# A new hand-written order for a recurrence and a token-mixing MLP on one core: pair 0's v and k are loaded ahead of q, and the cast of wk reads at a stride

## The chip, the core and the metric

The kernel runs on one core of a Trainium2 chip. The core has a matmul engine (PE, with its weight loads shown apart as PEld), a vector engine (DVE), a scalar engine (ACT), a general engine (POOL), and SP, which here only issues DMAs. Each engine takes its instructions strictly in the order of its own queue. The metric is the device time of one execution in microseconds (us); the time before is the median of three runs.

## What is computed

Per head, a linear attention with a decaying state; its output, heads side by side, is the input of a mixing layer over tokens. Batch 4, 8 heads, 768 tokens, head size 64, so the model width is 512; `d_hyper` is 64.

```python
gamma = 1.0 - 2.0 ** (-5.0 - np.arange(H))
for t in range(S):
    state = gamma * state + einsum('bhd,bhe->bhde', k[:, :, t], v[:, :, t])
    y[:, :, t] = scale * einsum('bhd,bhde->bhe', q[:, :, t], state)
x = y.transpose(0, 2, 1, 3).reshape(B, S, H * D)
wq, wk = x @ w_q, x @ w_k
W_tok = 1 / sqrt(d_hyper) * einsum('bsd,btd->bst', wq, wk)
mixed = einsum('bst,btd->bsd', W_tok, x)
return np.maximum(mixed, 0.0) @ w_out
```

## The kernel before

The recurrence is done in chunks of 128 tokens. Two chunks make a pair, three pairs a batch, twelve pairs (0 to 11) the whole. Inside a chunk the scores of q and k are masked and multiplied with v; what came before the chunk enters through the state. The mixing layer needs no 768 x 768 matrix: per batch it forms z, which is wk's transpose times x, and then multiplies it with wq.

All sums of PE go to eight banks. Bank 7 holds the running state; banks 0 to 6 are given to the steps by hand. Inputs land in 27 slots of a buffer called `stage` (one 512 KB load each), and outputs leave from slots too.

The order of everything is one string, `ORDER`. A word in it is a step, with its pair, its part, the engine behind a colon (A for ACT, V for DVE, P for POOL) or the banks behind an @ (a letter a or b after them takes half of two banks), and a slot behind =. So `cv.0.1:P` scales chunk part 1 of v of pair 0 on POOL, and `trk.2@12a` transposes k of pair 2 into halves of banks 1 and 2. A loop at the end of the kernel runs through the words and issues each step's instructions, so every engine's queue has them in the order of the words. Waits are set where data or a bank needs them. The steps, in the order in which one pair meets them, with the lines of the kernel before:

- `Lk Lq Lv` load k, q, v of a pair (L193, L172; v of kind M in four DMAs at L185; kind N at L178), `LW` the two small weights (L200), `LO` a half of w_out (L207).
- `ck cq` cast k and q to bf16, `cv` scales v by decay factors and casts (L419; L400 for kind 2; L410 for kinds M and N). Casts and copies are at L147 on ACT and at L148 on DVE and POOL.
- `trk trq` transpose k and q on PE, wide (8 matmuls, one bank) or split (16 small ones, halves of two banks); `ek eq` copy the result out.
- `sc` scores (L597, L583 for kind 2), half the heads each; `eat` masks them (L615, DVE).
- `st` adds a chunk to the state (L631); `es` copies the state out.
- `in` the state's share of the output (L670), `ia` the masked scores times v (L724, L710 for kind 2), `ex` scales both to x (L745, DVE).
- `xt` and `exT` transpose x; `W` casts w_q and w_k (in `W`, the second at L344), `WO` a half of w_out.
- `wqk` gives wq and wk of a pair (L787, L798), `ew` copies them out as m; `zm` and `ez` z of a batch (L824); `mx` the mixing (L843), `r` the relu (L861 on ACT, L863 on DVE), `pj` the output projection (L868), `eo` copies it to a slot, `S` stores it (L218).
- `fill` issues matmuls on a tile of zeros that nothing reads (L355).

`KINDS` has a letter for each pair: how its k and v lie on the partitions. R reads two tokens of 64 floats as one row, 2 keeps these pairs of tokens side by side through the whole step, M lays v out so that one instruction scales a part, N takes tokens in plain order. The load named by `FIRST` is issued ahead of the string, in two halves, one from ACT's queue and one from SP's.

Of the kernel before, what the change touches and what calls it, by code (L numbers as in the profile page):

```python
# [17 lines left out]
Lq.2=6 ck.0.1:A trq.0@0 eq.0:A trk.0@1 Lk.2=7 cq.1.0:A ek.0:A ck.1.1:A fill.11@2 sc.0.1@01 st.0.0
ck.1.0:P es.0.0:A Lv.2=8 cv.1.1:P cq.2.1:P Lk.3=9 Lq.3=10 cv.1.0:P eat.0.1:V LW=11 Lv.3=12 cq.2.0:P
trq.1@2 trk.1@34a st.0.1 sc.0.0@56 cv.2.0:P ek.1:V eat.0.0:V cv.2.1:P fill.4@0 in.0.1@01 cq.3.0:P  # L20
Lk.4=13 ck.3.0:P eq.1:A sc.1.0@23 sc.1.1@45 ck.2.1:A ck.2.0:A Lq.4=14 es.0.1:V eat.1.0:V ia.0.1@01
fill.1@6 st.1.0 ia.0.0@01 fill.3@6 trq.2@6 es.1.0:V eat.1.1:V fill.2@2 trk.2@5 eq.2:A ek.2:A
in.1.1@34 st.1.1 LO.0=15 fill.2@2 sc.2.1@56 cv.3.0:P ck.4.0:P cv.3.1:P Lv.4=16 es.1.1:A ex.0:V
LO.1=17 eat.2.1:V sc.2.0@01 st.2.0 in.1.0@34 eat.2.0:V xt.0@2 cq.3.1:A es.2.0:A ck.3.1:A exT.0:A
Lk.5=18 W:A cv.4.1:P fill.1@5 ia.1.1@34 cv.4.0:P ia.1.0@34 in.2.1@56 ia.2.0@56 ex.1:V ia.2.1@56
trq.3@0 in.2.0@56 fill.1@1 xt.1@4 wqk.0@3 eq.3:A trk.3@2 Lq.5=19 ex.2:V exT.1:V ck.4.1:A ek.3:V
xt.2@01a exT.2:V wqk.1@4 fill.1@5 sc.3.1@56 sc.3.0@01 ew.1:A cq.4:A wqk.2@2 ew.0:V Lv.5=20 Lq.6=21
Lk.6=22 Lv.6=23 ew.2:A cq.5:P eat.3.0:V eat.3.1:V st.3.0 zm.0.0@3 zm.0.1@3 trk.4@01a Lq.7=24 trq.4@2
cv.5.0:P ek.4:V WO.0:A ez.0:A es.3.0:A mx.1@34 r.1.0:A cv.5.1:P WO.1:A ia.3.1@56 Lk.7=25 in.3.1@56
ia.3.0@56 st.3.1 ck.6.0:P mx.0@01 eq.4:V r.1.1:V r.0:A Lq.8=26 sc.4.0@23 pj.1.0@4 Lv.7=0 es.3.1:V  # L30
ex.3:V ck.5.0:A ck.5.1:A pj.0.1@0 eo.0.1:A=1 Lk.8=3 eo.1.0:V=2 xt.3@1 eat.4.0:V pj.1.1@4 exT.3:V
sc.4.1@23 mx.2@56 st.4.0 trq.5@0 es.4.0:A trk.5@1 cv.6.0:P st.4.1 ck.7.0:P eat.4.1:V r.2.1:V
eo.1.1:A=2 ek.5:A r.2.0:A cv.6.1:P ia.4.0@34 ia.4.1@34 in.4.1@34 in.4.0@34 Lv.8=4 Lk.10=5 eq.5:V
es.4.1:V pj.0.0@2 cq.8.1:P sc.5.1@56 sc.5.0@01 cq.6:A eo.0.0:A=1 st.5.0 ex.4:V eat.5.1:V eat.5.0:V
ck.6.1:A es.5.0:A Lq.10=6 trq.6@3 pj.2.1@2 xt.4@6 cv.7.0:P cv.7.1:P ck.8.1:P exT.4:V in.5.0@45
in.5.1@45 ia.5.1@45 ia.5.0@45 Lq.9=7 eo.2.1:A=8 eq.6:V wqk.3@2 trk.6@01a wqk.4@3 ex.5:V xt.5@45a
cq.7:A ew.3:A ew.4:A Lk.9=10 st.6.0 ek.6:V exT.5:V sc.6.0@01 eat.6.0:V pj.2.0@6 eo.2.0:V=8 ck.7.1:A
es.6.0:A wqk.5@5 trq.7@01a trk.7@34a ew.5:A sc.6.1@56 zm.1.0@2 cv.8.0:P zm.1.1@2 Lv.9=9 ek.7:V
eq.7:A cq.8.0:A ez.1:A eat.6.1:V sc.7.0@01 st.6.1 mx.3@23 in.6.1@45 r.3.0:A es.6.1:A r.3.1:A
eat.7.0:V ck.10.0:P ia.6.0@45 ia.6.1@45 trq.8@6 ex.6:V cq.10.1:P cv.8.1:P st.7.0 mx.4@01 sc.7.1@23  # L40
ck.8.0:A eat.7.1:V xt.6@4 pj.3.1@5 eq.8:V eo.3.1:V=11 es.7.0:A r.4:A Lq.11=13 ia.7.0@23 ia.7.1@23
in.7.0@23 in.7.1@23 trk.8@01a ex.7:V exT.6:A Lv.10=14 pj.3.0@6 cq.9:P st.7.1 ek.8:A sc.8.0@01
sc.8.1@23 es.7.1:V eo.3.0:A=11 eat.8.0:V mx.5@45 st.8.0 r.5.1:A es.8.0:V r.5.0:V pj.4.1@6 ck.10.1:A
eo.4.1:A=15 wqk.6@0 cq.10.0:A pj.4.0@1 eat.8.1:V ew.6:V ck.9.1:P cv.9.0:P trk.10@6 cv.9.1:P
trq.10@45a xt.7@23a cv.10.0:P Lk.11=12 eo.4.0:A=15 eq.10:V exT.7:V in.8.0@01 in.8.1@01 ia.8.0@01
ia.8.1@01 cv.10.1:P pj.5.0@4 trq.9@5 ek.10:A ex.8:V eq.9:V ck.9.0:A ck.11.0:P Lv.11=17 sc.10.1@23
trk.9@01a pj.5.1@6 eo.5.0:A=16 cv.11.0:P ek.9:A xt.8@45a eat.10.1:V eo.5.1:V=16 sc.9.1@01 eat.9.1:V
sc.9.0@23 cq.11.0:A eat.9.0:V exT.8:A st.9.0 wqk.7@6 wqk.8@4 cq.11.1:A cv.11.1:P ew.7:A es.9.0:A
sc.10.0@01 zm.2.0@6 ew.8:A st.9.1 zm.2.1@6 es.9.1:A ez.2:A trq.11@23a st.10.0 eat.10.0:V in.9.1@45
es.10.0:A ck.11.1:A mx.8@01 eq.11:V r.8.1:V ia.9.0@45 ia.9.1@45 ia.10.1@23 r.8.0:A st.10.1  # L50
in.10.1@23 trk.11@01a in.10.0@23 ia.10.0@23 pj.8.1@6 ex.9:V ek.11:A sc.11.0@01 es.10.1:A ex.10:V
eo.8.1:A=18 sc.11.1@45 xt.9@23a eat.11.0:V st.11.0 pj.8.0@6 exT.9:A es.11.0:A S.3 eat.11.1:V mx.6@01
in.11.0@23 in.11.1@23 r.6.1:A eo.8.0:A=18 ia.11.0@23 r.6.0:V ia.11.1@23 mx.7@45 xt.10@01a ex.11:V
pj.6.1@6 exT.10:A xt.11@2 exT.11:A wqk.9@3 wqk.10@0 ew.10:A eo.6.1:A=19 r.7.1:A r.7.0:V wqk.11@2
ew.9:V pj.6.0@3 ew.11:A zm.3.0@6 zm.3.1@6 eo.6.0:A=19 ez.3:V pj.7.1@2 mx.10@01 r.10.0:V mx.11@56
mx.9@34 eo.7.1:A=21 pj.7.0@2 r.10.1:A pj.10.1@0 S.0 S.4 eo.7.0:A=21 r.11.0:A pj.10.0@1 eo.10.1:A=20
eo.10.0:A=20 S.5 S.8 S.2 r.11.1:V S.6 pj.11.1@2 S.1 r.9:V S.7 eo.11.1:V=22 pj.11.0@0 pj.9.0@1 S.10.1
# [19 lines left out]
def kernel(  # L77
# [255 lines left out]
    wqk_sb = const_pool.tile([128, NDM, 3 * DH], BF16, name="wqk_w")  # L333
    wout_sb = const_pool.tile([128, NDM, DM], BF16, name="wout_sb")

    def W(e):
# [6 lines left out]

        nc.scalar.mul(  # L344
            out=wqk_sb[:, :, 2 * DH :].rearrange("p a (u t) -> p a t u", u=U),
            in_=st[:, 1].rearrange("p a (t u) -> p a t u", u=U),
            mul=float(wk_scale),
        )

# [593 lines left out]
```

## Time and profile before

| | |
|---|---|
| median of 3 runs | 96.33 us (95.49 to 97.65) |
| the profiled execution | 96.55 us, of which the profile's span is 94.8 |
| granted TensorE clock | 0.994 |
| HBM read, written | 20.19 MB, 6.29 MB |

The profile shows one execution. A span's start is 0 us, and "busy" leaves out waiting, branches and DMA issues. A matmul's shown time holds its passage through the array, so several that follow each other overlap; the chain that ended last gives them at the pace at which they follow. In the timeline a row merges neighbours of one kind (x is their count), and the bracket tells how long the engine had been idle and what ended that. POOL's busy time lies between 6 and 71 us, PE's last matmul ends at 91.15.

### The profile page before, as it was taken

How to read it: one execution, taken by the hardware profiler on the slowest of the kernel's cores; microseconds unless marked ns; L12 is line 12 of the kernel's file. 1: busy time of each engine (PE TensorE's matmuls, PEld its weight loads, DVE VectorE, ACT ScalarE, POOL GpSimd, SP SyncE). 2: the span in 40 equal slices, each digit the busy share in tenths (PEclk: the TensorE clock that was granted, in tenths of full speed). 3: DMA queues.
4: the chain of work that ended last, by engine and by line, in shares of the span. 5: the costliest groups of instructions: out<-in, count | busy, mean ns of one | idle time of the engine just before them, and what ended most of it. 6: DMA issues, size and time to landing. Idle time of an engine off the chain costs nothing.

```text
span 94.8 us, 3658 instructions
## 1 busy us (share of the span) xinstructions
PE 84.8 (89%) x1537; PEld 56.7 (60%) x1553; DVE 74.3 (78%) x132; ACT 72.2 (76%) x119; POOL 54.7 (58%) x70
## 2 busy tenths in 40 slices
PE   4989399989989999999999999999999799999940
PEld 1335076657777745868877765676876577644410
DVE  6941999939879999999989998989999976142700
ACT  4444682989999998999687997998977578856450
POOL 6030069599996996999999989999880000000000
PEclk9999999999999999999999999999999999999997
DMA  0999999999999999999679999979599307447983
GB/s 23 321 306 352 318 338 335 325 332 275 335 345 337 359 356 355 293 365 331 129 216 340 392 351 289 323 160 229 126 390 399 142 7 296 154 185 290 406 335 116
DMA packets 38960, 26.71 MB, mean 282 GB/s; under 512 B 10272, under 2 KB 32800, under 8 KB 38944
## 3 DMA queue, kind: packets, MB, share of 16 engines
q1 hardware_dynamic: 38416, 26.22, 87.8%
q10 hardware_dynamic: 528, 0.26, 0.9%
q8 instruction: 12, 0.20, 0.9%
q14 instruction: 4, 0.03, 0.1%
HBM read 20.19 MB, written 6.29 MB: 279 GB/s over the span
## 4 chain that ended last, share of the span: by engine, by line
PE 62%; SPq 14%; DMA 7%; ACT 5%; issue 5%; DVE 4%; DVEq 0%
PE banks L868 22%; SPq L193 10%; DMA stage<-in_q_dram 7%; PE banks L787 6%; PE banks L724 5%; SPq L172 5%; PE banks L597 5%; PE banks L631 3%; PE banks L798 3%; PE banks L843 3%; PE banks L824 3%; PE banks L670 2%; PE banks L546 2%; DVE at L615 2%; PE banks L760 2%
## 5 line engine op out<-in xcount | busy, mean ns | idle before, releaser
L419 POOL TENSOR_TENSOR vs<-stage,fv 64x512 bf16<-64x512 f32 x28 | 29.2, 1043 | 4.2 <-DMA stage<-in_v_dram 1.9
L615 DVE TENSOR_TENSOR at<-banks,maskR 128x1024 bf16<-128x1024 f32 x20 | 23.9, 1218 | 2.3 <-PE banks L597 1.8
L868 PE MATMUL banks<-wout_sb,relu 128*128 128x512 bf16 x85 | 22.1, 381 | 0.7 <-issue 0.3
L147 ACT CAST ks<-stage 64x512 bf16<-64x512 f32 (+1 forms) x26 | 16.0, 616 | 3.4 <-DMA stage<-in_k_dram 3.1
L745 DVE TENSOR_TENSOR x<-banks,fy 128x1024 bf16<-128x1024 f32 x12 | 14.6, 1220 | 0.6 <-PE banks L670 0.3
L147 ACT COPY stage<-banks 128x512 f32<-128x512 f32 x19 | 11.2, 588 | 3.6 <-PE banks L868 3.5
L148 POOL CAST ks<-stage 64x512 bf16<-64x512 f32 (+1 forms) x16 | 9.9, 620 | 5.8 <-DMA stage<-in_k_dram 5.0
L868 PEld LDWEIGHTS <-relu 128*128 128x128 bf16 x96 | 8.1, 98 | 8.4 <-ACT relu L861 0.4
L355 PE MATMUL banks<-warm 128*128 128x512 bf16 x36 | 10.9, 439 | 1.4 <-DVE warm L226 1.2
L597 PE MATMUL banks<-qT,kT 64*128 64x128 bf16 x176 | 7.7, 218 | 1.9 <-ACT kT L147 1.8
L861 ACT ACTIVATE relu<-banks 128x512 bf16<-128x512 f32 (+1 forms) x12 | 8.1, 674 | 1.5 <-PE banks L843 1.5
L863 DVE TENSOR_SCALAR relu<-banks 128x512 bf16<-128x512 f32 (+1 forms) x9 | 6.7, 746 | 3.0 <-PE banks L868 1.8
L147 ACT CAST qs<-stage 128x512 bf16<-128x512 f32 (+1 forms) x9 | 6.9, 763 | 2.3 <-DMA stage<-in_q_dram 2.2
L148 POOL CAST qs<-stage 128x512 bf16<-128x512 f32 (+1 forms) x8 | 6.0, 748 | 4.2 <-DMA stage<-in_q_dram 3.8
L597 PEld LDWEIGHTS <-kT 64*128 64x128 bf16 x176 | 5.2, 94 | 4.9 <-ACT kT L147 3.2
L147 ACT COPY kT<-banks 128x1024 bf16<-128x1024 bf16 x7 | 7.1, 1017 | 1.2 <-PE banks L504 1.0
L724 PE MATMUL banks<-vs,at 128*128 128x64 bf16 x176 | 7.4, 194 | 0.1
L355 PEld LDWEIGHTS <-warm 128*128 128x128 bf16 x41 | 4.1, 109 | 5.7 <-issue 2.4
L147 ACT COPY xT<-banks 128x1024 bf16<-128x1024 bf16 x6 | 6.1, 1014 | 1.8 <-DVE at L615 1.1
L787 PE MATMUL banks<-xT,wqk_w 128*128 128x256 bf16 x48 | 7.2, 274 | 0.0
L147 ACT COPY qT<-banks 128x1024 bf16<-128x1024 bf16 x5 | 5.4, 1079 | 1.9 <-PE banks L546 1.8
L724 PEld LDWEIGHTS <-at 128*128 128x128 bf16 x176 | 5.9, 98 | 1.3 <-issue 0.4
(87 smaller groups left out, 143.5 us busy)
## 6 DMA issues: line engine op xcount, KB each, us to landing
stage<-in_q_dram SPq DMA_DIRECT2D x12, 512.0 KB, 6.9
stage<-in_k_dram SPq DMA_DIRECT2D x10, 512.0 KB, 6.3
stage<-in_v_dram SPq DMA_DIRECT2D x9, 512.0 KB, 7.0
out_dram<-stage SPq DMA_DIRECT2D x9, 512.0 KB, 4.0
out_dram<-stage SPq DMA_DIRECT2D x6, 256.0 KB, 2.1
stage<-in_moe_w_out_dram SPq DMA_DIRECT2D x4, 256.0 KB, 5.2
stage<-in_v_dram SPq DMA_DIRECT2D x8, 128.0 KB, 5.8
stage<-in_k_dram SPq DMA_DIRECT2D x3, 256.0 KB, 4.8
```

Source lines behind the costliest of these rows:

```text
L147: return nc.scalar.copy(out=out, in_=in_)
L148: return ENGINES[e].tensor_copy(out=out, in_=in_)
L193: eng.dma_start(out=to[g, hs], in_=fr[g, hs])
L355: nc.tensor.matmul(out=bank32(b), lhsT=warm[:, 0:128], rhs=warm, start=True, stop=True)
L419: eng.tensor_tensor(out=st["vs"][rows(j), c].rearrange("p hp x d -> p (hp x) d"), in0=src[rows(c), :, j], in1=fv[rows(c), cp, :, j].to_bro ...
L597: nc.tensor.matmul(out=at[:, x, hi, c], lhsT=kT[rows(x), hp, c], rhs=qT[rows(x), c, hp], start=(hi == 0 and c == 0), stop=(hi == 1 and c = ...
L615: ENGINES[e].tensor_tensor(out=st["at", half].rearrange("p x hi j t -> p x (hi j t)").rearrange("p x (n f) -> p x n f", n=n), in0=st["at_p ...
L724: nc.tensor.matmul(out=y[:, x, c, hp, :], lhsT=at[:, x, hi, c, :], rhs=vr[:, c, hp, x, :], start=first(p, x), stop=False, skip_group_check ...
L745: ENGINES[e].tensor_tensor(out=dst, in0=src, in1=f.to_broadcast([128, 2, H, D]), op=ALU.mult)
L787: nc.tensor.matmul(out=ps[:, 128:384], lhsT=wqk_sb[:, a, 0 : 2 * DH], rhs=st["xT"][:, a].rearrange("p c t -> p (c t)"), start=(a == 0), st ...
L861: nc.scalar.activation(out=dst, in_=src, func=ACT.Relu)
L868: nc.tensor.matmul(out=bank32(b[0]), lhsT=st["relu"][:, a // 2, a % 2, c * C : c * C + C], rhs=wout_sb[:, a, :], start=(a == 0), stop=(a = ...
```

## The change

`ORDER` is replaced as a whole, `FIRST` and two letters of `KINDS` change, and the cast of wk is written with its two views turned: before, it read wk in order and wrote at a stride; now it reads every eighth element and writes in order.

```diff
 ORDER = """
-fill.15@6 Lq.0=1 ck.0.0:V Lv.0=2 cq.0.1:V cq.0.0:P Lq.1=3 Lk.1=4 cv.0.1:V cq.1.1:V cv.0.0:V Lv.1=5
...
+fill.15@6 Lk.0=1 Lq.0=2 Lk.1=3 Lv.1=4 Lq.1=5 cv.0.0:P ck.0.0:A Lk.2=6 Lq.2=7 cq.0:A ck.0.1:V
...
-KINDS = "R2RRRRRMRRMN"
-FIRST = ('k', 0, 0)
+KINDS = "R2RRRRRRRMMN"
+FIRST = ('v', 0, 0)
...
         nc.scalar.mul(
-            out=wqk_sb[:, :, 2 * DH :].rearrange("p a (u t) -> p a t u", u=U),
-            in_=st[:, 1].rearrange("p a (t u) -> p a t u", u=U),
+            out=wqk_sb[:, :, 2 * DH :].rearrange("p a (u t) -> p a u t", u=U),
+            in_=st[:, 1].rearrange("p a (t u) -> p a u t", u=U),
```

Every line number behind the string is one less in the new kernel (L147 becomes L146).

By engine: POOL gets both `cv` of pair 0 (four instructions, DVE before), one of the two `WO`, and the casts of all of q of pairs 2 and 11 and of k of pair 11, and gives other casts of k and q away. DVE has two more `ek`, one more `eq`, two more `exT`, three more `es`, two more `eo`, one `ew` less, and five halves of relu less. ACT has these the other way round; its relus are eight whole pairs and three halves (before two and ten). PE has 35 fillers where it had 41; of the transposes 20 are wide in both.

Three places. The first is SP's queue, from the first load on (`stage` is the buffer of slots). Before:

```order
L193 DMA stage<-in_k_dram 128x4x128
L172 DMA stage<-in_q_dram 128x2x512
L193 DMA stage<-in_v_dram 128x8x128
L172 DMA stage<-in_q_dram 128x2x512
L193 DMA stage<-in_k_dram 128x8x128
L193 DMA stage<-in_v_dram 128x8x128
L172 DMA stage<-in_q_dram 128x2x512
```

In this queue as it is now, the same stretch reads:

```order
L192 DMA stage<-in_v_dram 128x4x128
L192 DMA stage<-in_k_dram 128x8x128
L171 DMA stage<-in_q_dram 128x2x512
L192 DMA stage<-in_k_dram 128x8x128
L192 DMA stage<-in_v_dram 128x8x128
L171 DMA stage<-in_q_dram 128x2x512
L192 DMA stage<-in_k_dram 128x8x128
L171 DMA stage<-in_q_dram 128x2x512
```

The first row is a half load in both (the other half is on ACT's queue). Pair 0 came as k, q, v and pair 1 as q, k, v; now they come as v, k, q and k, v, q. Ahead of the fourth pair's q stand now the two small weights.

The second is ACT's queue behind its table load and the decay factors, where pairs 0 and 1 begin (`ks` and `qs` are the casts of k and q, `kT` and `qT` their transposes). Before:

```order
L147 CAST ks<-stage 64x512 x2
L147 COPY qT<-banks 128x1024
L147 CAST qs<-stage 128x8x64
L147 COPY kT<-banks 128x1024
L147 CAST ks<-stage 128x8x64
```

Now, at the same place in ACT's queue:

```order
L146 CAST ks<-stage 64x512 x2
L146 CAST qs<-stage 128x2x8x64
L146 COPY kT<-banks 128x1024
L146 CAST ks<-stage 128x4x2x2x64
L146 CAST qs<-stage 128x8x64
L146 COPY kT<-banks 128x1024
```

The cast of all of q of pair 0 stands now between k's cast and the copy of kT; the copy of qT went to DVE.

The third is POOL's queue (`vs` is the scaled v). Before, from the first cast to the scalings of pair 4:

```order
L148 CAST qs<-stage 128x8x64
L148 CAST ks<-stage 128x8x64
L400 TENSOR_TENSOR vs<-stage,fv 128x8x64
L148 CAST qs<-stage 128x8x64
L400 TENSOR_TENSOR vs<-stage,fv 128x8x64
L148 CAST qs<-stage 128x8x64
L419 TENSOR_TENSOR vs<-stage,fv 64x512 x4
L148 CAST qs<-stage 128x8x64
L148 CAST ks<-stage 64x512 x2
L419 TENSOR_TENSOR vs<-stage,fv 64x512 x2
L148 CAST ks<-stage 64x512 x2
L419 TENSOR_TENSOR vs<-stage,fv 64x512 x6
```

POOL's queue now, from pair 2 to pair 5:

```order
L418 TENSOR_TENSOR vs<-stage,fv 64x512 x4
L147 CAST qs<-stage 128x8x64
L147 CAST ks<-stage 64x512 x2
L418 TENSOR_TENSOR vs<-stage,fv 64x512 x2
L147 CAST qs<-stage 128x8x64
L418 TENSOR_TENSOR vs<-stage,fv 64x512 x4
L147 CAST wout_sb<-stage 128x1024
L418 TENSOR_TENSOR vs<-stage,fv 64x512 x2
L147 CAST qs<-stage 128x2x8x64
L418 TENSOR_TENSOR vs<-stage,fv 64x512 x4
```

Ahead of that stand now four scalings of pair 0, two of pair 1, and two casts of q. The cast of a half of w_out stands between the two halves of pair 4's v; before, those halves followed pair 3's directly and both halves of w_out were ACT's.

On PE, `trk.2` stands now between the two `sc.1`, the first fillers are 15 and 3 ahead of `trk.0`, and six more follow `trq.0`, ahead of `st.0.1` and `sc.0.0`. Before the last projections the order is the same kind as it was: behind `zm.3.1` come pj.7.1, the three `mx` of pairs 9 to 11, and seven `pj`.

More of the change, by code (lines that the diff above doesn't have):

```diff
@@ L16 @@
 ORDER = """
-fill.15@6 Lq.0=1 ck.0.0:V Lv.0=2 cq.0.1:V cq.0.0:P Lq.1=3 Lk.1=4 cv.0.1:V cq.1.1:V cv.0.0:V Lv.1=5
[L18 to L57, printed above, removed]
```

41 lines of the change are left out of this document (40 added, 1 removed).

## The prediction

> **What bounds the kernel now.** I read the page first, then the engines' busy time in windows, then the chain that ended last, then the timeline of the first 34 us. From the page (share of the span, then tenths of each of 40 slices of 2.37 us):
>
> ```profile
> PE 84.8 (89%) x1537; PEld 56.7 (60%) x1553; DVE 74.3 (78%) x132; ACT 72.2 (76%) x119; POOL 54.7 (58%) x70
> ...
> PE   4989399989989999999999999999999799999940
> DVE  6941999939879999999989998989999976142700
> POOL 6030069599996996999999989999880000000000
> ```
>
> The windows (PE, PEld, DVE, ACT, POOL busy, granted clock, DMA share, GB/s):
>
> ```profile
> 0.00:14.80 14.80, 11.49 (x101) 5.63 (x102) 10.38 (x57) 7.86 (x13) 4.46 (x14) 1.00 0.88 279
> 14.80:33.80 19.00, 17.73 (x417) 13.51 (x421) 16.28 (x21) 16.84 (x26) 16.45 (x19) 1.00 1.09 330
> 33.80:91.20 57.40, 55.53 (x1023) 37.61 (x1032) 47.62 (x57) 46.96 (x81) 33.74 (x38) 1.00 0.86 271
> ```
>
> The chain (start, us, what), with the ramp, what single steps take on PE there, and the tail:
>
> ```profile
> 14.68 6.53 DMA stage<-in_q_dram
> ...
> 25.07 1.25 ACT wqk_w L344
> 26.37 0.39 PE banks L798 x8
> ...
> 29.17 0.54 PE banks L787 x4
> 29.72 0.23 PE banks L798 x8
> ...
> 30.20 0.73 PE banks L824 x12
> ...
> 37.09 0.33 PE banks L597 x8
> ...
> 38.43 0.45 PE banks L498 x8
> ...
> 41.56 0.24 PE banks L631 x8
> ...
> 84.98 4.64 PE banks L868 x21
> ```
>
> Up to 26.4 us the chain is loads and casts; behind that it is almost all PE. From the first output projection at 33.8 to the end of PE's work (the 3.6 us behind 91.2 are the last copy and store) PE is busy 55.53 of 57.40 us, so only 57.40 - 55.53 = 1.87 us of gaps are there to win. The matmuls themselves are the same in both kernels: same pairs, same eight R, one 2, two M and one N layout, and twenty wide transposes in both. So the new time is the old one, less the lead (or lag) with which PE reaches its first output projection, plus any waits the new order makes after it. The rest of this is these two numbers.
>
> **Part 1: the loads.** In SP's queue (its rows stand with the change) pair 0's v moves from third to first, its k from first to second, its q from second to third, and v of pair 1 ahead of its q. When a place in that queue lands is read where an engine stood waiting for it (timeline; the bracket is idle time and what ended it):
>
> ```profile
> 5.92 0.86 POOL L148 CAST qs<-stage 128x512 bf16<-128x512 f32 x1 [3.65 <-DMA stage<-in_q_dram]
> 9.01 1.39 DVE L419 TENSOR_TENSOR vs<-stage,fv 64x512 bf16<-64x512 f32 x2 [2.69 <-DMA stage<-in_v_dram]
> 10.29 0.62 ACT L147 CAST qs<-stage 128x512 bf16<-128x512 f32 x1 [1.78 <-DMA stage<-in_q_dram]
> 11.81 0.81 POOL L148 CAST ks<-stage 128x512 bf16<-128x512 f32 x1 [5.03 <-DMA stage<-in_k_dram]
> 13.38 1.05 POOL L400 TENSOR_TENSOR vs<-stage,fv 128x512 bf16<-128x512 f32 x1 [0.76 <-DMA stage<-in_v_dram]
> 14.63 0.61 POOL L148 CAST qs<-stage 128x512 bf16<-128x512 f32 x1 [0.20 <-DMA stage<-in_q_dram]
> 16.10 2.50 ACT L147 CAST ks<-stage 64x512 bf16<-64x512 f32 x4 [1.98 <-DMA stage<-in_k_dram]
> 17.80 4.38 POOL L419 TENSOR_TENSOR vs<-stage,fv 64x512 bf16<-64x512 f32 x4 [1.00 <-DMA stage<-in_v_dram]
> ```
>
> So places 2 to 9 land at 5.9, 9.0, 10.3, 11.8, 13.4, 14.6, 16.1 and 17.8, about 1.5 us apart, but for 3.1 between the second and third. All loads of this stretch are 512 KB and the DMA share is 1.09, so I let each place keep its time whatever tensor it carries. Thus k0 lands at 5.9, q0 at 9.0, q1 at 13.4, k2 at 14.6.
>
> **Part 2: the start.** Durations (the column is mean ns), and at the end three rows of the timeline:
>
> ```profile
> L419 POOL TENSOR_TENSOR vs<-stage,fv 64x512 bf16<-64x512 f32 x28 | 29.2, 1043 | 4.2 <-DMA stage<-in_v_dram 1.9 <-DVE at L615 0.7
> L147 ACT COPY kT<-banks 128x1024 bf16<-128x1024 bf16 x7 | 7.1, 1017 | 1.2 <-PE banks L504 1.0
> L148 DVE COPY qT<-banks 128x1024 bf16<-128x1024 bf16 x7 | 4.8, 682 | 0.5 <-PE banks L550 0.5
> L147 ACT CAST qs<-stage 128x1024 bf16<-128x1024 f32 x3 | 3.1, 1046 | 0.1
> L419 DVE TENSOR_TENSOR vs<-stage,fv 64x512 bf16<-64x512 f32 x4 | 2.7, 684 | 2.7 <-DMA stage<-in_v_dram 2.7
> ...
> 7.74 2.54 PE L355 MATMUL banks<-warm 128*128 128x512 bf16 x11
> ...
> 12.37 1.23 DVE L615 TENSOR_TENSOR at<-banks,maskR 128x1024 bf16<-128x1024 f32 x1 [0.23 <-issue]
> ...
> 29.22 2.35 DVE L615 TENSOR_TENSOR at<-banks,maskR 128x1024 bf16<-128x1024 f32 x2
> ```
>
> ACT's queue now has cq.0 (both halves, 1.05) ahead of ek.0: q0 at 9.0, cast to 10.05, kT copied by 11.1. PE transposes q0 by 10.55 (sixteen small ones now; the eight large of L498 take 0.45), DVE copies it by 11.25. Behind the transposes stand six fillers (2.54/11 = 0.23 each, 1.4) and st.0.1 (0.24), so the first scores come at 12.2 and the first mask at 12.4: the same as the 12.37 before. The fillers cost nothing only because qT and kT are late anyway.
>
> From there DVE carries the ramp. To the end of ex.2 it has six masks and three x of 1.22 - 0.09 (two masks take 2.35 and not 2.44), four copies of 0.59 and two states of about 0.33: 10.2 + 2.4 + 0.7 = 13.3. It waits some 1.5 more, chiefly for pair 2: its k lands at 14.6, ACT reaches it at 14.8 behind ek.1, casts 2.50 to 17.3, and PE's trk.2, which stands in front of sc.1.1, holds PE idle meanwhile. So ex.2 ends near 27.2. Then PE's xt.2 (0.34, an estimate from sixteen small against eight large transposes), DVE's ew.0 and exT.2 to 28.4, PE's two sc.3 meanwhile, wqk.2 (0.54 + 0.23) to 29.2, trq.4 (0.45), and both zm.0, whose twelve matmuls take 0.73 to 0.9 with ew.2 on ACT between: 30.5.
>
> **Part 3: the wk cast.** Rows for it, and for ACT reading at a stride and in order:
>
> ```profile
> L344 ACT ACTIVATE wqk_w<-stage 128x256 bf16<-128x256 f32 x1 | 1.3, 1338 | 0.0
> L147 ACT CAST m<-banks 128x384 bf16<-128x384 f32 x9 | 4.4, 485 | 1.5 <-PE banks L798 1.4
> L147 ACT CAST z<-banks 128x256 bf16<-128x256 f32 x3 | 1.1, 372 | 0.0
> ```
>
> The m cast reads its bank at a stride and writes in order, as the wk cast now will: 485 ns for 384 elements, 113 above z's 372 for 256 read in order, or 0.88 ns an element. So a strided read from a bank is free, and 256 elements would take some 0.4 us: 0.94 saved. But wk lies in SBUF, which that row does not show; the other end is that it takes 1.34 still, or more. I take 0.4. [...] The walk puts ACT's exT.0 at 21.5 to 22.5, then a q cast 0.63, a state 0.3 and the w_q cast 0.62 (as the q cast of the same size): W ends at 24.5 with a wk cast of 0.4 and at 25.4 with 1.34, and PE comes to wqk.0 only at 25.7, behind in.2.1: nothing gained or lost either way.
>
> **Part 4: to the first projection.** ACT casts ck.4.0 from 29.7 (behind ew.2) to 31.0, then z and, of the same shape, a state (0.37 less overlap, 0.3 each), half of w_out (1.05, as the q cast of the same size) and relu.1 (0.95, as a kT copy less overlap): 33.6. POOL does the other half of w_out by then. With sc.4.0 and sc.4.1 in front, pj.1.0 starts near 34.0.
>
> ```profile
> 33.77 2.00 PE L868 MATMUL banks<-wout_sb,relu 128*128 128x512 bf16 x7
> ```
>
> That is 0.23 later than before, but with st.4.0 (0.24) and sc.4.1 (0.33) done already, which came after it: a lead of 0.57 - 0.23 = 0.34.
>
> **Part 5: behind it.** Summed over the whole, POOL takes over the four scalings of v0 (4 x 1.04 = 4.2) and a w_out half (1.05) and gives back casts (about 1.8); DVE loses those four (2.7) and takes copies from ACT instead. Following both queues and the banks, I find PE waiting twice. mx.2 writes bank 4, which holds pair 3's transposed x until exT.3: ACT gets there by 33.6 + relu 0.95 + state 0.3 + two k casts 1.25 + exT.3 0.95 = 37.1, PE by 34.0 + two pj 1.7 + xt 0.45 + st 0.24 + two in 0.36 = 36.75: a wait of about 0.4. And sc.5.1 needs ek.5, which ACT ends at 37.1 + 1.25 + relu 0.95 + 0.95 = 40.3, while PE, from 37.15 on with mx, two ia, trq, trk, pj and st (some 2.8), comes at 39.95: 0.3. With scraps elsewhere 0.9 in all, against at most 1.87 of gaps before. Such a walk overlooks waits, so I credit 0.2 and no more. The tail is alike: seven projections one behind the other, then copy and store.
>
> **The sum.** 0.34 + 0.2 = 0.54: span 94.8 - 0.5 = 94.3. The profiled execution took 96.55, 1.75 beyond its span, and lies 0.22 above the median of the runs, 96.33. So 96.33 - 0.54 = 95.8.
>
> **Rivals.** *The start comes early.* If the gap of 3.1 us between places 2 and 3 is not the place's but v0's own, q0 lands at 7.4 and the first scores come at 7.4 + 1.05 + 0.5 + 1.4 + 0.24 = 10.6, 1.6 earlier. For it: all other steps are 1.2 to 1.7. Against it: k1, k2 and v2 land no earlier. With 1.5 of lead kept to the projection and 0.5 of gaps, 96.33 - 2.0 = 94.3; with all 1.87 of gaps gone, 93.0. Here PE wants wqk.0 by 24.2, and if the wk cast still takes 1.34, W ends at 25.4 less 1.0 and up to 0.3 of this lead goes. [...]
>
> *POOL sets the pace (the slower side).*
>
> ```profile
> 30.51 4.35 POOL L419 TENSOR_TENSOR vs<-stage,fv 64x512 bf16<-64x512 f32 x4 [0.66 <-DVE at L615]
> ...
> stage<-in_moe_w_out_dram SPq DMA_DIRECT2D x4, 256.0 KB, 5.2
> ```
>
> The w_out cast now stands between v4's halves. If v4 lands near 30.5 as before, POOL ends cv.4.0 at 32.6 (4.35/2 for a half pair) and PE wants it at 32.8 (34.0 less two scores, two fillers and 0.1); cv.4.1 ends at 35.9 and PE wants it at 36.2; cv.5.0 has 0.7 in hand. So from a delay of 0.3 on PE waits for POOL, and behind the cast of w_out queue cv.4.1, cq.5 and cv.5, for which st.4.1, trq.5 and ia.5 wait on PE, and behind those everything. POOL does 2.2 us for each half of an R pair and is full to pair 9, so it doesn't catch up. A landing 2 to 3 us late (the step of 3.1 above is 1.6 late by itself), or waits of 0.1 to 0.2 at each of the seven pairs 3 to 9 that I overlooked, cost 2.5 to 3: 96.33 + 2.6 = 98.9. For it: all engines are at 9 tenths from 30 to 65 us, and a fixed order pays any error in full. Against it: POOL begins to scale with the first load and not at 13.4, so only landings can make it late.
>
> *Nothing moves.* The ramp is the loads' and ends as before; a lead under 0.3 vanishes in the first waits: 96.3.
>
> **Numbers.** The forecast has 0.42, nothing moves 0.08, the early start 0.20, POOL 0.30. Two per cent, 1.9 us, is about what a measurement of this kernel can tell from no change: 94.4 to 98.3. That gives faster 0.20, same 0.50, slower 0.30. The range goes from 93.3, inside the early start's ends, to 99.6, POOL's case with another 0.7; the forecast alone has 94.9 to 96.8.
>
> **What would show it.** Right: first mask at 12.4, first L868 at 33.5 to 34.2, PE busy over 55 of the 57 us behind it. The early start shows as a first mask before 11.5. POOL's case shows as PE idle before L631 or L724 with a POOL releaser between 32 and 60 us. The wk cast is shown by its own row, 0.4 or 1.3. I am wrong on all counts if ACT or DVE, not POOL, starves PE in the middle, or if loads land in other steps than by place.

## The result: half a per cent faster

| | before | after |
|---|---|---|
| median of 21 runs each | 96.08 us (95.21 to 100.11) | 95.45 us (95.01 to 98.54) |
| ratio after to before, 95% interval | | 0.9946 (0.9920 to 0.9971) |

The forecast was 95.8 us. By the bound of 2% this is no change, but the interval lies below 1.

Comparisons leave disturbed runs out; the execution profiled with the result was one (97.45 us), so the lines of after below are from another execution of the same kernel (95.49 us, span 93.7; the second run of the experiments). Shares of its span, and tenths of PE's 40 slices:

```profile
PE 85.7 (91%) x1547; PEld 57.2 (61%) x1547; DVE 74.9 (80%) x130; ACT 68.7 (73%) x111; POOL 58.2 (62%) x71
...
PE   4994999799899999999999999999999999999940
```

Its windows (PE, PEld, DVE, ACT, POOL, clock, DMA share, GB/s):

```profile
0.00:14.80 14.80, 12.25 (x102) 5.72 (x103) 9.15 (x52) 8.82 (x14) 8.58 (x17) 1.00 0.91 296
...
14.80:33.80 19.00, 17.64 (x432) 13.94 (x431) 18.14 (x22) 14.75 (x25) 16.83 (x18) 1.00 1.09 336
33.80:91.20 57.40, 55.85 (x1024) 37.52 (x1018) 47.66 (x57) 45.13 (x74) 32.81 (x37) 1.00 0.86 272
```

What changed is what the diff says: in the first 14.8 us POOL works 8.58 us where it had 4.46. In PE's row the 3 of the fifth slice is gone, where PE stood in front of its first scores (a 4 stands in the fourth instead), and so is the 7 of the 32nd, the slice from 73.5 to 75.8 us.

The start, from the timeline, with idle time and its end in brackets:

```profile
6.61 1.25 ACT L146 CAST ks<-stage 64x512 bf16<-64x512 f32 x2 [3.12 <-DMA stage<-in_k_dram]
6.61 2.22 DVE L147 CAST ks<-stage 64x512 bf16<-64x512 f32 x2 [1.89 <-DMA stage<-in_k_dram]
...
7.93 1.04 ACT L146 CAST qs<-stage 128x1024 bf16<-128x1024 f32 x1
...
9.49 1.01 ACT L146 COPY kT<-banks 128x1024 bf16<-128x1024 bf16 x1 [0.51 <-PE banks L497]
...
10.29 1.47 PE L354 MATMUL banks<-warm 128*128 128x512 bf16 x6
...
10.40 0.69 DVE L147 COPY qT<-banks 128x1024 bf16<-128x1024 bf16 x1 [0.24 <-PE banks L549]
...
11.94 0.40 PE L596 MATMUL banks<-qT,kT 64*128 64x128 bf16 x8
...
12.43 1.23 DVE L614 TENSOR_TENSOR at<-banks,maskR 128x1024 bf16<-128x1024 f32 x1 [1.34 <-PE banks L596]
```

First mask at 12.43, as before (12.37) and as forecast (12.4). What holds it up is what the forecast's times implied and its words denied: kT is there at 10.50, qT at 11.09, and PE is still in its six fillers until about 11.7. The chain that ended last has the fillers, and ahead of them DVE's casts of k0 (start, us, what):

```profile
6.61 1.03 DVE ks L147
7.65 1.19 DVE ks L147
8.89 0.56 PE banks L497 x7
10.36 1.40 PE banks L354 x6
```

The first projection, and PE's last matmuls, both from the timeline:

```profile
34.17 1.04 PE L867 MATMUL banks<-wout_sb,relu 128*128 128x512 bf16 x4
```

```profile
83.84 6.22 PE L867 MATMUL banks<-wout_sb,relu 128*128 128x512 bf16 x28
```

From first projection to PE's end it takes 90.06 - 34.17 = 55.9 us. Before it was 91.15 - 33.77 = 57.4. So the start gives next to nothing here, and the gain is behind it: the reverse of how the forecast had split it.

Other profiles say the same. One of the old order with only the cast of wk changed (an experiment below) is of an execution of 96.18 us, close to the median of before. PE's timeline at its first projections and at its end:

```profile
32.82 1.04 PE L868 MATMUL banks<-wout_sb,relu 128*128 128x512 bf16 x4
34.15 1.04 PE L868 MATMUL banks<-wout_sb,relu 128*128 128x512 bf16 x4 [0.29 <-ACT relu L861]
...
84.55 6.22 PE L868 MATMUL banks<-wout_sb,relu 128*128 128x512 bf16 x28
```

It is 1.35 us ahead of after at the first projection and 0.71 behind at PE's end. Over all profiles taken, first projection to PE's end takes 57.0 to 57.9 us in five of the old order. In nine of the new order it takes 55.9 to 56.0 in seven, and 56.6 and 56.9 in the two that have a stop of 0.9 in it. Of the difference 0.57 is work that the new order does ahead of the first projection (st.4.0 and sc.4.1).

### The profile page after: what moved, and what is told of

It is laid out like the page before. It is cut to its first block, busy times and chain, and to the rows that moved or that the text cites. A ratio compares the mean times of both kernels' runs of the same rounds, so it can differ in the third digit from the quotient of the medians.

```text
span 95.6 us, 3651 instructions
## 1 busy us (share of the span) xinstructions
PE 86.7 (91%) x1547; PEld 57.5 (60%) x1547; DVE 75.1 (78%) x130; ACT 68.7 (72%) x111; POOL 58.2 (61%) x71
## 4 chain that ended last, share of the span: by engine, by line
PE 69%; ACT 12%; DMA 5%; issue 5%; DVE 4%; SPq 0%; DVEq 0%
PE banks L867 20%; PE banks L786 6%; PE banks L596 6%; PE banks L723 6%; DMA stage<-in_k_dram 5%; ACT ks L146 5%; PE banks L630 4%; ACT relu L860 3%; PE banks L545 3%; PE banks L823 3%; PE banks L842 3%; PE banks L797 3%; PE banks L497 3%; PE banks L354 2%; DVE ks L147 2%
## 5 line engine op out<-in xcount | busy, mean ns | idle before, releaser
L418 POOL TENSOR_TENSOR vs<-stage,fv 64x512 bf16<-64x512 f32 x32 | 33.6, 1050 | 6.1 <-DMA stage<-in_v_dram 4.1
L867 PE MATMUL banks<-wout_sb,relu 128*128 128x512 bf16 x96 | 23.8, 380 | 0.0
L146 ACT CAST ks<-stage 64x512 bf16<-64x512 f32 (+1 forms) x29 | 18.3, 632 | 3.3 <-DMA stage<-in_k_dram 2.8
L146 ACT COPY stage<-banks 128x512 f32<-128x512 f32 x17 | 9.9, 588 | 4.3 <-PE banks L867 4.1
L860 ACT ACTIVATE relu<-banks 128x1024 bf16<-128x1024 f32 (+1 forms) x11 | 9.9, 913 | 1.4 <-ACT relu L860 0.7
L146 ACT CAST qs<-stage 128x512 bf16<-128x512 f32 (+1 forms) x9 | 6.9, 764 | 2.4 <-DMA stage<-in_q_dram 2.4
L147 POOL CAST qs<-stage 128x512 bf16<-128x512 f32 (+1 forms) x9 | 6.7, 755 | 3.0 <-DMA stage<-in_q_dram 1.8
L146 ACT CAST m<-banks 128x384 bf16<-128x384 f32 x10 | 4.7, 482 | 5.3 <-PE banks L797 5.1
L147 POOL CAST ks<-stage 64x512 bf16<-64x512 f32 (+1 forms) x11 | 7.2, 651 | 2.1 <-DMA stage<-in_k_dram 1.6
L630 PEld LDWEIGHTS <-ks 128*64 128x64 bf16 (+1 forms) x176 | 4.4, 110 | 4.4 <-issue 2.1
L630 PE MATMUL banks<-vs,ks 128*64 128x64 bf16 (+1 forms) x176 | 6.6, 200 | 0.0
L147 DVE COPY stage<-banks 128x512 f32<-128x512 f32 x7 | 4.8, 684 | 1.9 <-PE banks L867 1.2
```

The costliest lines, as they stand in the source:

```text
L146: return nc.scalar.copy(out=out, in_=in_)
L147: return ENGINES[e].tensor_copy(out=out, in_=in_)
L418: eng.tensor_tensor(out=st["vs"][rows(j), c].rearrange("p hp x d -> p (hp x) d"), in0=src[rows(c), :, j], in1=fv[rows(c), cp, :, j].to_bro ...
L630: nc.tensor.matmul(out=state_ps[rows(x), hp, :], lhsT=st["ks"][rows(c), hp, j, x, :] if two else st["ks"][:, c, hp, x, :], rhs=st["vs"][ro ...
L860: nc.scalar.activation(out=dst, in_=src, func=ACT.Relu)
L867: nc.tensor.matmul(out=bank32(b[0]), lhsT=st["relu"][:, a // 2, a % 2, c * C : c * C + C], rhs=wout_sb[:, a, :], start=(a == 0), stop=(a = ...
```

## The experiments

Each job ran the kernel before beside its own runs, on one chip (its median 96.17 us in the first job, 96.08 to 96.32 in the later ones). "Slack" below is the time at which a step starts on PE, less the work that PE has done until then: it rises by each wait.

### What is the noise, and does the gain hold? (no edit)

> The kernel before, unchanged, for a second profile of it: 96.1 us, a ratio of 1.00. Every theory expects the same; if its first output projection starts more than 0.5 us away from 33.8, single profiles can't show a lead of 0.3.

> The changed kernel, unchanged, for a profile that is not disturbed: 95.5 us, a ratio near 0.995, span near 93.6. If the gain is a lead from the ramp, the first output projection stands at or before 34.3 with st.4.0 and sc.4.1 done; if the gain comes behind the ramp, it starts later than 34.5 and PE's gaps from there to the end are under 1 us.

The copy of before: 97.31 us, ratio 1.0138 (1.0080 to 1.0196), from six runs, three of them with a mean granted clock of 0.976 to 0.982. The kernel after: 95.49 us, 0.9946 (0.9913 to 0.9980). So the gain came out a second time with the same number, but an identical kernel can differ by 1.4% when it has few runs: half a per cent is only as good as its repeats. The copy's profile has its first projection at 34.10 and PE's end at 91.49, 57.4 us as before. So the split above is not the luck of one profile. By the sign set beforehand, a first projection at 34.17 with st.4.0 and sc.4.1 done would be a lead from the ramp; the stretch behind it, 0.9 shorter after those 0.57 are taken off, says that most of the gain is not.

### The cast of wk alone, in both kernels

```diff
-            out=wqk_sb[:, :, 2 * DH :].rearrange("p a (u t) -> p a t u", u=U),
-            in_=st[:, 1].rearrange("p a (t u) -> p a t u", u=U),
+            out=wqk_sb[:, :, 2 * DH :].rearrange("p a (u t) -> p a u t", u=U),
+            in_=st[:, 1].rearrange("p a (t u) -> p a u t", u=U),
```

The first kernel is before with this edit; the second is after without it.

> The order before with only the cast of wk changed. There the chain of waits runs through this cast into wqk.0 at 26.37. If the cast is the gain: its 0.66 us come off, 95.5 (ratio 0.993 to 0.995). If the order is the gain: PE has too little behind wqk.0 that could start earlier, 96.0 to 96.1 (ratio 0.998 to 1.001).

> The new order with the old cast of wk, 1.34 us. By the prediction PE comes to wqk.0 later than the cast ends, so nothing is lost: 95.5 (ratio 0.995). If the cast is the gain: 96.0 to 96.1 (ratio 0.999 to 1.001).

Before with the new cast: 96.15 us, 1.0017 (0.9981 to 1.0052). After with the old cast: 95.67 us, 0.9971 (0.9934 to 1.0007). ACT's timeline around the cast, new order with the new cast, then with the old:

```profile
24.56 0.69 ACT L343 ACTIVATE wqk_w<-stage 128x256 bf16<-128x256 f32 x1
25.66 1.01 ACT L146 COPY kT<-banks 128x1024 bf16<-128x1024 bf16 x1 [0.41 <-ACT wqk_w L343]
```

```profile
24.35 1.35 ACT L343 ACTIVATE wqk_w<-stage 128x256 bf16<-128x256 f32 x1
25.57 1.01 ACT L146 COPY kT<-banks 128x1024 bf16<-128x1024 bf16 x1
```

The cast is 0.66 us shorter, and ACT then stands idle for 0.41: kT's copy starts at the same time in both. In the old order the cast alone gives nothing, and in the new one it ends ahead of an idle stretch, so it isn't where the time came from. Whether it carries 0.2% in the new order the intervals can't tell. The second profile also has this row on PE, a wait that the forecast had foreseen at this place with 0.4:

```profile
38.06 0.38 PE L842 MATMUL banks<-m,z 64*128 64x256 bf16 x3 [0.94 <-ACT xT L146]
```

### The loads of pair 0 back in the order k, q, v; the rest new

```diff
-fill.15@6 Lk.0=1 Lq.0=2 Lk.1=3 Lv.1=4 Lq.1=5 cv.0.0:P ck.0.0:A Lk.2=6 Lq.2=7 cq.0:A ck.0.1:V
+fill.15@6 Lq.0=1 Lv.0=2 Lk.1=3 Lv.1=4 Lq.1=5 cv.0.0:P ck.0.0:A Lk.2=6 Lq.2=7 cq.0:A ck.0.1:V
...
-FIRST = ('v', 0, 0)
+FIRST = ('k', 0, 0)
```

> The new order with pair 0 loaded as k, q, v again; all else as in the changed kernel. v0 lands third, near 8.5, so POOL scales its first part until 10.7 and its second until 12.9; st.0.0 and st.0.1 stand in PE's queue ahead of trq.0 and sc.0.0, so the first scores move from 11.9 to 13.1. If a lag at the first scores is carried to the end: 96.2 to 96.7 (ratio 1.002 to 1.007). If the loads of pair 2 level it: 95.5 to 95.8 (0.994 to 0.998).

99.14 us, with the first scores at 15.40, later than I had worked out. One of the six runs, with a mean clock of 0.997, took 97.05 us; the others had 0.979 to 0.983. That is too few for an interval. PE's timeline, then windows with the clock in the column behind POOL's:

```profile
11.35 0.42 PE L630 MATMUL banks<-vs,ks 128*64 128x64 bf16 x8 [4.02 <-POOL vs L418]
...
13.19 2.04 PE L354 MATMUL banks<-warm 128*128 128x512 bf16 x5 [0.33 <-issue]
...
15.40 0.40 PE L596 MATMUL banks<-qT,kT 64*128 64x128 bf16 x8
```

```profile
7.00:11.00 4.00, 0.33 (x6) 0.27 (x4) 0.00 (x0) 1.51 (x2) 1.78 (x2) 1.00 1.10 303
11.00:15.40 4.40, 3.72 (x38) 1.78 (x39) 1.11 (x2) 1.17 (x2) 4.19 (x6) 0.61 1.08 360
```

With v0 last, PE stands 4 us in front of st.0.0, which waits for POOL's scaling of v0. Then the granted clock is 0.61, and a filler takes 0.41 instead of 0.24 us. First scores come 3.5 us later than in after, and in this execution the lag stays to the end (98.93 us); in the one that kept the clock about 1.6 us are left of it. So in the *new* order v must come first, because st.0.0 now stands ahead of the first scores on PE. The new order of PE needs the new order of the loads; the new loads under the old order of PE were not tried.

### k of pair 0 whole on ACT

```diff
-fill.15@6 Lk.0=1 Lq.0=2 Lk.1=3 Lv.1=4 Lq.1=5 cv.0.0:P ck.0.0:A Lk.2=6 Lq.2=7 cq.0:A ck.0.1:V
+fill.15@6 Lk.0=1 Lq.0=2 Lk.1=3 Lv.1=4 Lq.1=5 cv.0.0:P ck.0.0:A Lk.2=6 Lq.2=7 cq.0:A ck.0.1:A
```

The row above shows two DVE casts of k0 in 2.22 us; before, the same two took 0.85. In after POOL scales v0 meanwhile. The run just above (k, q, v) settles whether that is the reason: it has the same steps on DVE and POOL, but v0 comes late, and POOL has nothing to scale while DVE casts. Its timeline:

```profile
4.72 0.86 DVE L147 CAST ks<-stage 64x512 bf16<-64x512 f32 x2
...
9.14 4.38 POOL L418 TENSOR_TENSOR vs<-stage,fv 64x512 bf16<-64x512 f32 x4 [6.88 <-DMA stage<-in_v_dram]
```

The two casts take 0.86 us there, as before. What moving one of the parts to ACT does:

> The new order with the second part of k0 cast on ACT and not on DVE. In the changed kernel DVE's two casts take 2.24 us beside POOL's scalings, 0.85 before beside none. If POOL holds DVE there, on ACT they take 1.25, trk.0 ends at 8.9 or earlier and q0's cast starts 0.3 later (ACT is in order): 95.5 to 95.8, ratio 0.994 to 0.998. If the 2.24 was on the way to the first scores: 94.9 to 95.2 (ratio 0.988 to 0.991).

98.39 us, with a ratio of 1.0101 (1.0021 to 1.0182) from only two of the six runs, 96.71 and 97.51 us, the two with a mean clock of 0.996 or more. I had overlooked ACT's queue: ck.0.1 stands behind cq.0 there.

```profile
8.05 1.04 ACT L146 CAST qs<-stage 128x1024 bf16<-128x1024 f32 x1 [0.39 <-DMA stage<-in_q_dram]
9.12 1.24 ACT L146 CAST ks<-stage 64x512 bf16<-64x512 f32 x2
```

PE waits 2.48 us for it, and in the profiled execution the clock falls to 0.66 (in the windows, the column behind POOL's):

```profile
10.00:15.00 5.00, 4.25 (x47) 2.12 (x50) 1.11 (x2) 2.94 (x4) 2.66 (x3) 0.66 1.08 359
```

The two casts take 1.24 us on ACT. What a k0 cast unhindered on DVE would be worth at the end this run doesn't show, because it puts the cast behind cq.0.

### The half of w_out back on ACT

```diff
-mx.1@23 in.3.1@01 ek.4:V ex.3:V mx.0@45 WO.0:P r.1:A Lv.6=23 r.0:A cv.4.1:P st.4.0 fill.2@6
+mx.1@23 in.3.1@01 ek.4:V ex.3:V mx.0@45 WO.0:A r.1:A Lv.6=23 r.0:A cv.4.1:P st.4.0 fill.2@6
```

> The new order with the cast of w_out's second half on ACT and not on POOL. ACT stands on the way to the first projection, so by the prediction's walk the projection comes 1.05 later, 35.2 for 34.2: 96.0 to 96.6 (ratio 1.000 to 1.006). If POOL set the pace in the new order, its 1.05 less would show: 95.0 or less (ratio under 0.990).

96.26 us, 1.0013 (0.9981 to 1.0045): the gain is gone. PE's timeline:

```profile
34.31 0.62 PE L596 MATMUL banks<-qT,kT 64*128 64x128 bf16 x16 [1.01 <-ACT relu L860]
34.86 1.04 PE L867 MATMUL banks<-wout_sb,relu 128*128 128x512 bf16 x4
```

ACT's relu comes one cast (1.05) later and PE waits 1.01 for it; the first projection is 0.7 later. POOL, where that cast stands in after, has room for it:

```profile
30.77 1.04 POOL L147 CAST wout_sb<-stage 128x1024 bf16<-128x1024 f32 x1 [0.21 <-DMA stage<-in_moe_w_out_dram]
31.89 2.15 POOL L418 TENSOR_TENSOR vs<-stage,fv 64x512 bf16<-64x512 f32 x2
```

It ends v4's second half by 34.04; st.4.1, which needs it, starts at 36.45. The move to POOL is right, and the rival "POOL sets the pace" has no ground in these traces.

### The pause before 75 us, and the place in PE's stream

The three profiles of the old order so far have a pause inside pair 9's transposes of x, between the twelfth and the thirteenth matmul, that no other engine ends. Before:

```profile
74.03 0.35 PE L760 MATMUL banks<-identity,x 64*128 64x64 bf16 x12
74.98 0.24 PE L760 MATMUL banks<-identity,x 64*128 64x64 bf16 x4 [0.60 <-issue]
```

Fillers early on shift everything behind them in PE's stream. First six fewer in the old order, then six more in it; then six more in the new one:

```diff
-Lq.2=6 ck.0.1:A trq.0@0 eq.0:A trk.0@1 Lk.2=7 cq.1.0:A ek.0:A ck.1.1:A fill.11@2 sc.0.1@01 st.0.0
+Lq.2=6 ck.0.1:A trq.0@0 eq.0:A trk.0@1 Lk.2=7 cq.1.0:A ek.0:A ck.1.1:A fill.5@2 sc.0.1@01 st.0.0
```

> The order before with six fillers fewer ahead of sc.0.1 (5 for 11), so 35 as in the changed kernel; PE waits there for kT in any case. In three profiles of the order before PE pauses 0.8 us inside xt.9, at the same matmul, 12 of its 16, and waits for nothing that is shown. If the pause hangs on the place in PE's instruction stream, it moves or goes: 95.3 to 95.6 (ratio 0.992 to 0.995) if it goes altogether. If it belongs to xt.9 or to the stores at that time, it stays at the same matmul: 96.1 (ratio 1.00).

96.94 us, ratio 1.0018 (0.9970 to 1.0067). The pause is gone from that place, but PE now stands idle ahead of its first scores (timeline), and the clock drops to 0.66 behind that (windows):

```profile
12.14 0.40 PE L597 MATMUL banks<-qT,kT 64*128 64x128 bf16 x8 [2.89 <-ACT kT L147]
```

```profile
12.00:17.00 5.00, 4.73 (x86) 3.22 (x91) 3.92 (x5) 2.67 (x5) 3.96 (x5) 0.66 1.08 339
```

Ten of its twelve runs have a mean clock of 0.962 to 0.982, as do two of the 23 runs of before in the same job. So this run doesn't settle what the pause costs. And no break stands six matmuls later, where a place in the stream would put it.

```diff
-Lq.2=6 ck.0.1:A trq.0@0 eq.0:A trk.0@1 Lk.2=7 cq.1.0:A ek.0:A ck.1.1:A fill.11@2 sc.0.1@01 st.0.0
+Lq.2=6 ck.0.1:A trq.0@0 eq.0:A trk.0@1 Lk.2=7 cq.1.0:A ek.0:A ck.1.1:A fill.17@2 sc.0.1@01 st.0.0
```

> The order of before with 17 fillers instead of 11 ahead of the first scores; nothing else. PE waits for kT and qT until about 11.9 there anyway, so the six cost at most 6 x 0.22 = 1.3 us less the idle time they fill. Theory (the pause of about 0.8 us inside the transposes of x of pair 9 hangs on the place in PE's stream of instructions): with the stream shifted by six the pause is gone from that place or stands at another matmul; if it is gone and the start is not later, 0.6 to 1.0 us less than before, ratio 0.990 to 0.995; if the start is 0.6 later, ratio 0.998 to 1.003. Rival (the pause belongs to the work done there, or to the exT copy ahead of it): it stays at the thirteenth of the sixteen transposes of pair 9, and the ratio is 1.000 to 1.014.

96.21 us, 0.9978 (0.9936 to 1.0020). The same stretch of its timeline:

```profile
74.48 0.26 PE L760 MATMUL banks<-identity,x 64*128 64x64 bf16 x6
74.94 0.32 PE L760 MATMUL banks<-identity,x 64*128 64x64 bf16 x10 [0.20 <-issue]
```

Six matmuls more, with their weight loads, and the break stands exactly six matmuls earlier: behind the sixth, not the twelfth. In this profile, in the copy of before and in the one with the new cast, 1373 matmuls stand ahead of the break. So it goes with a place in PE's stream of instructions rather than with the work done there; but as the run with six fewer has none, the place alone doesn't make it. Its length is now 0.20 us; in time the shift is not told from nothing.

```diff
-fill.15@6 Lk.0=1 Lq.0=2 Lk.1=3 Lv.1=4 Lq.1=5 cv.0.0:P ck.0.0:A Lk.2=6 Lq.2=7 cq.0:A ck.0.1:V
+fill.21@6 Lk.0=1 Lq.0=2 Lk.1=3 Lv.1=4 Lq.1=5 cv.0.0:P ck.0.0:A Lk.2=6 Lq.2=7 cq.0:A ck.0.1:V
```

> The new order with 21 fillers instead of 15 at the very start, where PE waits for the first load (k at 6.3) anyway; the stream behind is six instructions later, the times of the ramp should not change (first scores 11.9, first projection at 34.2). Theory (the place in the instruction stream decides whether a pause of 0.8 to 1.1 us falls behind the projection): the change of place alone can bring such a pause, so the ratio is either 0.994 as before the shift, or 1.000 to 1.006 with a pause at one matmul that no other engine ended. Rival (the new order has fewer waits behind the projection because of its engines and banks alone): PE's slack grows by 0.3 to 0.5 from first projection to last, ratio 0.992 to 0.997, no pause.

95.45 us, 0.9941 (0.9913 to 0.9970), no pause behind the projection. Here the rival's expectation held: the new order keeps its gain when its stream is shifted.

### Five fillers fewer ahead of the first scores

```diff
-fill.3@0 trk.0@0 cv.0.1:P Lv.2=8 st.0.0 ek.0:A fill.1@1 trq.0@12a es.0.0:V Lk.3=9 LW=10 fill.6@3
+fill.3@0 trk.0@0 cv.0.1:P Lv.2=8 st.0.0 ek.0:A fill.1@1 trq.0@12a es.0.0:V Lk.3=9 LW=10 fill.1@3
```

> The new order with 1 filler instead of 6 between the transposes of q of pair 0 and its scores. By the prediction's words the six cost nothing because kT and qT are late anyway: first scores stay at 11.9. Rival one (in the profile kT is copied by 10.5 and qT by 10.8, and the fillers stand in front of the scores): first scores at 10.9 to 11.1; the ramp is then bound by the loads and DVE, as forecast, so the first projection stays at 34.0 to 34.2 and the ratio at 0.992 to 0.997. Rival two (the 0.9 us are kept to the end): first projection at 33.2 to 33.5, ratio 0.983 to 0.988. Rival three (without them PE's clock drops): first scores 10.9 or later, but PE's matmuls up to 15 us at 0.4 instead of 0.22 us each, and the first projection later than 34.4, ratio above 1.000.

> The kernel of the run before this one once more (1 filler instead of 6 ahead of the first scores), for a profile in which the granted clock stays at 1.00 through the ramp. If the time won at the first scores is kept, they stand at 10.4 to 10.6 (11.9 with six fillers), the first projection at 32.9 to 33.5 (34.2), the last ends at 88.2 to 88.9 (89.6), ratio 0.983 to 0.990. If the loads and DVE bind the ramp as forecast, the first projection is back at 34.0 to 34.2 and the ratio at 0.992 to 0.997, and the ratio of the run before was the luck of few runs. If fewer fillers bring the lower clock on, again about one run in three shows it and the profile too.

95.15 us, 0.9855 (0.9802 to 0.9909) from six runs; then 97.50 us, 0.9923 (0.9884 to 0.9962) from thirteen. The two medians differ so much because of the clock: ten of the 19 runs kept it and took 94.7 to 95.5 us (median 95.0; the ratios are theirs), and nine took 97.5 to 98.8 with a mean granted clock of 0.94 to 0.96. Of 45 runs with the six fillers in place (after twice, and the one with more at the start) four had a clock that low. Both profiles are of executions that lost it. The clock in 40 slices is 9 throughout with six fillers; in the two runs with one:

```profile
PEclk9999999855799999999999999999999999999999
```

```profile
PEclk9999999555579999999999999999999999999998
```

PE's timeline in the last of these, and its windows:

```profile
10.34 0.32 PE L630 MATMUL banks<-vs,ks 128*64 128x64 bf16 x8
10.87 0.40 PE L596 MATMUL banks<-qT,kT 64*128 64x128 bf16 x8 [0.22 <-DVE qT L147]
```

```profile
14.80:20.00 5.20, 4.38 (x108) 3.60 (x108) 3.79 (x5) 2.65 (x5) 4.26 (x5) 0.74 1.14 338
20.00:25.00 5.00, 5.00 (x78) 3.60 (x72) 3.52 (x4) 1.99 (x4) 4.53 (x6) 0.50 1.11 350
25.00:30.00 5.00, 5.00 (x92) 4.42 (x90) 3.74 (x6) 3.79 (x7) 4.66 (x6) 0.74 1.12 336
```

The first scores are 1.07 us earlier (10.87 for 11.94): the fillers do hold them up. Where the clock stays, about 0.4 us of that is left at the end (95.0 against 95.4 for the like runs of after); no profile shows where the rest went. Where it falls, the granted clock is 0.50 from 20 to 25 us in both profiles (the first has 0.84, 0.50 and 0.98 in the same three windows). With 0.50 as the low value all through, an estimate from these means, it is low from 18.3 to 25.2 us in the first and from 17.3 to 27.6 in the second. That starts 7 to 8 us behind the one filler that is left of the six (at 9.88 and 10.02), and the end is 2 to 3 us later. Over all runs this kernel did worse: mean 96.5 us for 19, against 95.8 for the 33 of after. In the old order six fillers fewer did lose the clock (ten of the twelve runs above, with 2.89 us idle in the profiled one). That the six here pay for themselves by keeping it fits this, but isn't shown. Thirteen of the 19 runs, with seven of the nine, were on a chip on which no run had the six; there before, with all its fillers, had a clock of 0.977 to 0.982 in five of 17 runs, and on the other three chips in six of 75. On one chip and in one job it is two of six with one filler against one of twelve with six. No version here beats the kernel after for certain.

## Why the prediction was right, point by point

*The time and its sign.* 95.8 forecast, 95.45 measured; 0.54 of gain forecast against 96.08 - 95.45 = 0.63. The two profiles differ by more, 94.8 - 93.7 = 1.1 of span, because the profile of before lay 0.47 above the median of its 21 runs and that of after 0.04. That the sum came out is in part luck: taken against the execution of 96.18 us above, the lead was 1.1 smaller than forecast and the gain behind it 1.3 larger.

*"I let each place keep its time whatever tensor it carries."* Wrong by about a microsecond. Waits in the timeline that a load ended:

```profile
11.03 1.05 POOL L399 TENSOR_TENSOR vs<-stage,fv 128x512 bf16<-128x512 f32 x1 [1.29 <-DMA stage<-in_v_dram]
...
12.20 0.62 ACT L146 CAST qs<-stage 128x512 bf16<-128x512 f32 x1 [0.75 <-DMA stage<-in_q_dram]
...
15.06 1.04 POOL L147 CAST qs<-stage 128x1024 bf16<-128x1024 f32 x1 [1.21 <-DMA stage<-in_q_dram]
16.56 1.04 POOL L418 TENSOR_TENSOR vs<-stage,fv 64x512 bf16<-64x512 f32 x1 [0.47 <-DMA stage<-in_v_dram]
```

k0 came at 6.6 (5.9 forecast), but v1 at 11.0 (11.8), q1 at 12.2 (13.4), q2 at 15.1 (16.1), v2 at 16.6 (17.8), and q0 at 7.9 at the latest (9.0). So the step of 3.1 us did not belong to the place, which is what the rival of an early start asked for; the profile taken with the result has q0 at 8.5, half way. With v0 third again (k, q, v) the step is back: q0's cast starts at 5.95, and POOL waits for v0 until 9.14. Why v0 takes that long there stays open. Yet the first scores came at 11.94, and not at the rival's 10.6: DVE's casts of k0 took 2.22 us for 0.85, so trk.0, which stands in front of trq.0, ended near 9.4, and q's cast, ready at 8.97, was transposed only from 9.95; then came the fillers. Two errors of about 1 us each cancelled, and the forecast time of the first mask was right by luck.

*"The fillers cost nothing only because qT and kT are late anyway."* Wrong. With qT there at 11.09 the scores stood behind the fillers and st.0.1 for 0.85 us. The forecast's own numbers said so: qT at 11.25, scores at 12.2. What it left out altogether is what the fillers may be for, the clock; the runs with fewer of them bear on that.

*DVE carries the ramp; wqk.0 at 25.7, zm.0 ended at 30.5.* wqk.0 started at 25.73 and zm.0 ended at 30.18, and DVE is busy 18.14 of the 19.00 us from 14.8. The chain that ended last runs mostly over PE there, so that DVE alone sets these times isn't shown. Of the microsecond that the loads were early little or nothing is left by then.

*The wk cast.* 0.4 forecast, 1.34 as the other end, 0.69 measured. 256 elements read at a stride from SBUF take 0.69 here, about 0.3 more than the 0.37 of 256 read in order from a bank, but far less than the strided write's 1.34. The forecast's 0.4 had the rate of the m cast, which reads from a bank; this read from SBUF doesn't reach it, and it doesn't stay near 1.34 either. The time hung on neither, as forecast.

*The lead at the first projection, 0.34.* It starts at 34.17 (34.0 forecast): 0.40 later than before, with 0.57 of work done already, so a lead of 0.17; against the copy's profile (34.10) it is 0.50, and against the old order with the new cast (32.82) it is a lag of 0.78. Profiles of one order differ by more than the term, so they neither confirm it nor refute it.

*Behind it, "I credit 0.2 and no more".* This term was mis-sized. From first projection to PE's end after takes 55.9 us and before 57.4: 1.5 less, of which 0.57 is the work moved ahead. Some 0.9 is left where 0.2 was credited. The 1.87 us of gaps, which the forecast took for all that could be won, were misread: the profile of before lacks 13 of the 1036 matmuls of that stretch, and a missing record looks like a gap. PE's idle time in that stretch is 0.45 in after; in the copy of before, 57.41 - 56.52 = 0.89:

```profile
34.09:91.50 57.41, 56.52 (x1036) 37.65 (x1032) 47.65 (x57) 46.90 (x81) 34.59 (x39) 1.00 0.87 275
```

```profile
34.17:90.10 55.93, 55.48 (x1011) 37.26 (x1008) 47.66 (x57) 44.19 (x74) 32.50 (x36) 1.00 0.86 271
```

So 0.44 is idle time; the pause at 75 us alone is 0.54 in the copy. The other half, 0.47, is a shorter busy time for the same steps (one more of the transposes is wide in after, and a wide one is slower: 0.61 us for its 8 matmuls in after's timelines, 0.41 for the 16 of a split one). So half of this gain is not in gaps at all, and the forecast had no term for it. That it is pace between neighbours of other kinds is my estimate from the windows' busy time, and was not shown. Of the two waits that the forecast walked out, sc.5.1 waits 0.2 for ACT's kT at 40.3 (0.3 forecast), and mx.2's shows only with the old cast.

*The rivals.* POOL never set the pace: w_out's cast is better there (the run with it on ACT loses 0.7%), and no PE wait behind the first projection in after ended with POOL. "Nothing moves" would be 1.000, outside the interval. "PE busy over 55 of the 57 us behind it": 55.85.

*What stays open.* Why single executions have pauses of about 1 us that no engine ends, at places that change from profile to profile (the one profiled with the result has 1.06 us at 26.46 and 0.88 at 60.16); why the profiled execution of before lies 0.47 above its median, which is what the profiles show beyond the medians; and whether the six fillers keep the clock.

## What to carry to other kernels

Read a filler in an order as work in the way of what stands behind it (here the first scores came 1.07 us earlier with five fewer), and look at the clock of what runs several us later: it was 0.50 from 20 to 25 us in both profiles with five fewer, though that the fillers had kept it up was not shown. Look at the spread of the runs, on more than one chip, and not only at the best of them before you take one out. Where the busiest engine is at 97% behind a ramp, a new order still won something in the busy time and the pauses of its stream, so don't credit gaps alone. A lead at one point is only worth what the end keeps of it: compare the stretch behind it too, in several profiles. And a step that is moved to another engine must be costed beside what its new neighbour does at that moment, not by its row from elsewhere.
